# Sizing TensorE's fill-in work in an attention and MLP kernel: when ScalarE's bank comes free, what runs first as a round ends, and an early half of the last projection

## The chip, the cores and the metric

The kernel runs on one core of a Trainium2 chip. The metric is the device time of one execution in microseconds (us). Before the change the median of three runs was 858.73 us (858.62 to 859.59). The span that a profile shows is some 1.8 us shorter than the time of the same run. Ratios are taken only between kernels that ran on the same chip in the same rounds.

Engines are named as the profile has them: PE is TensorE, DVE is VectorE, ACT is ScalarE, POOL is GpSimd, SP is SyncE. PSUM is the memory that TensorE writes its sums to; a piece of it that holds one tile of sums is called a bank here.

## The reference

One gate per token mixes the result of an attention block with that of an MLP block. All inputs are bf16.

```python
# x: (1, 2048, 512); 32 heads of 16
q, k, v = split_heads(x @ wqkv)
scores  = einsum("bhqd,bhkd->bhqk", q, k) * 16 ** -0.5
a = merge_heads(softmax(scores) @ v) @ wo

h  = gelu(layernorm(x) @ w1)                    # 512 -> 512
hs = shift_rows(h, by=(1, -1, 2, -2)) @ w2      # each quarter of the columns by its own shift
x1 = x + hs
b  = x1 + gelu(layernorm(x1) @ w3) @ w4         # 512 -> 1792 -> 512

g = sigmoid((x * gate_w).sum(-1))
return g * a + (1 - g) * b
```

Attention dominates: 32 heads times 2048 x 2048 scores. Each score needs an exponential, and no single engine could do all of them in time: at the 0.955 us that ScalarE takes for two tiles, the 2048 tiles would be 978 us of ScalarE (an estimate).

## The kernel before

The Python code holds a model of the engines. At build time it plays the program through, picks for each engine what to do next, and so lays down a fixed order of instructions; nothing is decided on the chip. Attention runs in 32 rounds (4 chunks of queries, 4 groups of 8 heads, 2 halves of a group), each of 64 score tiles of 128 x 512. A round's value matmuls sum into one PSUM bank, `acc`, which is copied out when the round ends; only then may the next round's value matmuls start, and only some ten of its score tiles may be issued ahead.

A score tile goes one of two ways. ScalarE takes two at a time and does a true exp. VectorE takes one at a time with a bit trick, then makes shifted copies (the third by POOL), so that four value matmuls together average out the trick's error. All other TensorE work is *fill-in*: the projections of attention and MLP, and value matmuls. It is put between the score groups. This is the heart of it, where TensorE picks its next work:

```python
def pe_pick():
    t = sim.t
    ...   # 1. scores, if a PSUM bank of ScalarE's or VectorE's is free and tiles may be issued
    if ops:
        sim.pe_run(ops)
        return True
    ...
    # 2. fill-in: how many passes of 216 ns?
    tr = sim.t_free["ACT"]                     # when ScalarE ends the instruction that it is at work on
    budget = tr - t - 95.0 + (SL[turn[0]])     # SL = (350, 350)
    if tr <= t:
        budget = 500.0
    n = int(budget // 216.0)
    if n <= 0:
        return False
    n = min(n, MAXU)                           # MAXU = 9
    ops = []
    g = gen_ready()                            # a projection whose inputs are there
    cnt = pv_counts()                          # value matmuls that are ready
    flush = n_left(min(acc_round[0], NR - 1)) == 0   # the round has no scores left to issue
    press = sum(cnt) > PRESS or len(sim.free["PA"]) <= PA_LOW or len(sim.free["PD"]) <= PD_LOW
    ...
    if g is not None and g.due <= sim.tiles:   # a projection that is due goes first, always
        do_gen()
    if press:
        do_pv(0.01)                            # value matmuls before projections
        do_gen()
    else:
        do_gen()
        if (len(ops) + 3) // 4 < n:
            do_pv(PV_FULL)
    if not ops and any(cnt):
        do_pv(0.01 if flush else PV_IDLE)
```

Two other places matter. The gate's sixteen columns are stored so that every element is on its own:

```python
d1 = dma(2200.0, [a], lambda: nc.sync.dma_start(
    out=zE_dram[:].rearrange("(t p) -> p t", p=P), in_=zE[:]))
```

And at the end, between the copy of the last sums and the steps that normalise them, TensorE does projections of the last chunk, which wait for nothing that is new:

```python
nc.scalar.copy(out=ab[:, 256:512], in_=acc[:, 256:512])
nc.vector.tensor_copy(out=ab[:, 0:256], in_=acc[:, 0:256])
for b in range(4):
    nc.tensor.matmul(pd[:, 4*b:4*b+4], lhsT=ab[:, b*P:(b+1)*P], rhs=idf[:, 0:P:32], start=True, stop=True)
# before these, in TensorE's order: last_gen(0..2); after them last_mms(3):
# each one fp32 identity matmul (adds y) and four passes with wo, G = 0..3
```

The whole kernel before:

The softmax here doesn't subtract the row's maximum and nothing guards it: scores larger than these inputs give would overflow.

## Time and profile before

| | before |
|---|---|
| span of the profiled run | 858.7 us |
| mean granted clock of TensorE | 0.962 |
| busy: PE, DVE, ACT, POOL | 93%, 91%, 86%, 44% |
| exp pairs on ScalarE | 717 |
| bit-trick tiles on VectorE | 615 |
| ScalarE idle ahead of its exps | 100.5 us |
| last copy of sums to the end | 14.7 us |

The lines of the page that carry this are in the prediction. How they are read: a group's line has the busy time, the mean time of one in ns, and then the idle time of that engine just before these instructions with what ended most of it. The waits give, for one waiting line and one releaser, the total, the number of times and the longest. A timeline line has start, length, engine and line, what it does, how many in a row, and in brackets how long the engine had been idle and what released it.

One thing that the prediction tells only by numbers is better seen. This is the timeline of before at a place with projections:

```profile
684.10 2.12 PE L495 MATMUL ring<-w,hT 128*32 128x512 bf16 x36
686.16 0.39 PE L789 MATMUL psA<-q,kT 32*128 32x512 bf16 x2
686.65 1.94 ACT L866 ACTIVATE PA<-psA 128x1024 bf16<-128x1024 f32 x2 [0.71 <-PE ring L789]
```

Thirty-six matmuls, four side by side, are nine passes. They take 2.12 us. ScalarE has two banks, each good for one exp of about 0.95 us, so it runs dry in that time and stands for 0.71 us until scores come again. When that run of fill-in ends both banks are empty.

The old budget counts until the instruction that ScalarE is at work on ends, and adds a quarter of a microsecond. The plan, built again with its picks printed, shows how nine passes come of it: they are three picks in a row, of two, three and four passes. The first is made while the model has ScalarE idle, the second during the first exp. The third comes just after that exp has ended; in the model its bank is free only 160 ns later, so no score can be issued yet, and the budget now counts to the end of the second exp, which already runs. While a GELU runs, the budget is cut only by `MAXU`.

### The profile page before, as it was taken

To read this page: it belongs to the slowest core of one execution; us is meant where nothing else is said; L and a number is where in the kernel's file an instruction comes from. 1 tells how busy PE (TensorE), PEld (TensorE's weight loads), DVE (VectorE), ACT (ScalarE), POOL (GpSimd) and SP (SyncE) were. 2 spreads that over 40 slices of the span, in tenths; PEclk is the share of its full clock that TensorE was granted. 3 is DMA by queue.
4 is the path that set the end of the run, shared out by engine and by line. 5 is a ranking of instruction groups with operands and counts; after the bars stand their busy time and mean duration, and the time that the engine had idled before them with its cause. 6 is when DMAs were issued, how large, how long until landed. Compare 5 with 4: busy or idle time off the path is not lost.

```text
span 858.7 us, 24104 instructions
## 1 busy us (share of the span) xinstructions
PE 794.5 (93%) x9715; PEld 253.8 (30%) x9715; DVE 785.6 (91%) x1657; ACT 735.1 (86%) x743; POOL 379.6 (44%) x369
## 2 busy tenths in 40 slices
PE   8979999998999898979999998999989999979987
PEld 3423333222222222222232232332222332222323
DVE  6978999998999999997969998999999989989893
ACT  6867788989899897998958998789999779999883
POOL 3243444444444453443524544344555534445442
PEclk9988999997899999998999997999989999989999
DMA  9212222113002232011000002101100100000000
GB/s 223 77 34 56 61 55 47 38 40 103 6 18 66 65 102 64 9 39 39 15 28 26 19 18 43 34 12 27 34 18 18 31 24 13 16 17 19 15 18 29
DMA packets 67016, 34.62 MB, mean 40 GB/s; under 512 B 46684, under 2 KB 62300, under 8 KB 66904
## 3 DMA queue, kind: packets, MB, share of 16 engines
q1 hardware_dynamic: 65288, 32.29, 14.9%
q8 instruction: 76, 1.25, 0.6%
q10 hardware_dynamic: 1616, 0.79, 0.3%
q14 instruction: 36, 0.29, 0.1%
HBM read 17.39 MB, written 6.81 MB: 28 GB/s over the span
## 4 chain that ended last, share of the span: by engine, by line
PE 41%; DVE 36%; ACT 11%; issue 5%; DMA 5%; SPq 1%; ACTq 0%; POOL 0%; DVEq 0%; POOLq 0%
PE acc L954 15%; PE ring L495 14%; DVE PD L891 14%; DVE PD L920 11%; PE psA L789 11%; ACT PA L866 7%; ACT hT L707 2%; DMA pk<-den 2%; DVE st L616 2%; DMA zE_dram<-zE 1%; DVE accsb L970 1%; DVE hT L706 1%; DVE x_sb L685 1%; DVE V L579 1%; DVE xn L636 1%
## 5 line engine op out<-in xcount | busy, mean ns | idle before, releaser
L866 ACT ACTIVATE PA<-psA 128x1024 bf16<-128x1024 f32 x717 | 684.4, 1029 | 100.5 <-PE ring L789 51.6
L923 POOL TENSOR_SCALAR PD<-PD 128x1024 uint16<-128x1024 uint16 x308 | 326.1, 1060 | 446.4 <-DVE PD L920 298.1
L891 DVE TENSOR_SCALAR PD<-ring 128x512 uint16<-128x512 f32 x615 | 400.9, 679 | 26.9 <-PE ring L789 18.9
L954 PE MATMUL acc<-PD,V 128*17 128x512 bf16 x2460 | 339.5, 395 | 21.1 <-DVE PD L920 7.4
L789 PE MATMUL psA<-q,kT 32*128 32x512 bf16 x1433 | 270.7, 392 | 23.8 <-ACT PA L866 22.4
L954 PE MATMUL acc<-PA,V 128*17 128x512 bf16 x1433 | 283.4, 388 | 0.4 <-DVE accsb L970 0.4
L920 DVE TENSOR_SCALAR PD<-PD 128x1024 uint16<-128x1024 uint16 x616 | 260.5, 464 | 1.8
L789 PE MATMUL ring<-q,kT 32*128 32x512 bf16 x615 | 201.7, 398 | 5.9 <-DVE PD L891 5.5
L789 PEld LDWEIGHTS <-kT 32*128 32x128 bf16 x2048 | 72.6, 91 | 286.0 <-issue 284.0
L954 PEld LDWEIGHTS <-V 128*17 128x17 bf16 x3893 | 94.3, 89 | 199.9 <-issue 160.8
L495 PE MATMUL ring<-xnT,w 128*32 128x512 bf16 x1152 | 84.8, 382 | 1.6 <-DVE PD L891 1.3
L495 PE MATMUL ring<-w,hT 128*32 128x512 bf16 x1152 | 81.3, 388 | 1.1 <-DVE PD L891 0.9
L495 PEld LDWEIGHTS <-w 128*32 128x32 bf16 x1920 | 45.3, 96 | 49.6 <-issue 32.9
L987 POOL TENSOR_TENSOR oT<-accsb,bcs 128x512 bf16<-128x512 f32 x31 | 40.6, 1311 | 9.4 <-DMA bcs<-rr 9.4
L495 PEld LDWEIGHTS <-hT 128*32 128x32 bf16 x1152 | 28.3, 97 | 37.7 <-issue 19.2
L706 DVE CAST hT<-ring 128x512 bf16<-128x512 f32 x56 | 38.1, 681 | 1.3 <-PE ring L495 0.9
L495 PE MATMUL ring<-w,w 128*32 128x256 bf16 (+1 forms) x768 | 36.2, 316 | 0.7 <-DVE PD L891 0.4
L707 ACT ACTIVATE hT<-hT 128x7168 bf16<-128x7168 bf16 x4 | 24.7, 6177 | 0.0
L970 DVE COPY accsb<-acc 128x512 f32<-128x512 f32 x31 | 21.1, 679 | 2.7 <-PE acc L954 2.7
L616 DVE BATCH_NORM_STATS2 st<-x_sb 128x6 f32<-128x512 bf16 x32 | 21.8, 681 | 0.0
L495 PE MATMUL ring<-wo,oD 128*32 128x512 bf16 x240 | 20.9, 380 | 0.0
L495 PE MATMUL ring<-w,wq 128*32 128x512 bf16 x256 | 18.4, 382 | 2.3 <-DVE PD L891 1.4
(82 smaller groups left out, 203.5 us busy)
## 6 DMA issues: line engine op xcount, KB each, us to landing
bcs<-rr SPq DMA_DIRECT2D x124, 64.0 KB
xn_dram<-xn SPq DMA_DIRECT2D x32, 128.0 KB
w<-in_B_w_dram SPq DMA_DIRECT2D x5, 512.0 KB
oD<-oT SPq DMA_DIRECT2D x124, 16.0 KB
w<-in_B_w_dram SPq DMA_DIRECT2D x4, 448.0 KB
out_dram<-ot SPq DMA_DIRECT2D x13, 128.0 KB
x_sb<-in_A_x_dram SPq DMA_DIRECT2D x3, 512.0 KB
w<-in_A_wqkv_dram SPq DMA_DIRECT2D x2, 256.0 KB
```

Of the source, the lines that this page charges most:

```text
L495: units.append([Op("col", j, lambda j=j, lf=lf, rf=rf, n0=n0, n1=n1, st=st, sp=sp: nc.tensor.matmul(get()[32 * j:32 * j + 32, n0:n1], lhsT ...
L616: a = dve(600, deps, lambda: nc.vector.bn_stats(out=sb.slot[:], in_=x_sb[:, t, :]), prio=6, at=at, acq=[sb])
L706: pre.append(evac(g, PSUM_NS, lambda ps, m=m: nc.vector.tensor_copy(out=h2[:, m, :], in_=ps[:])))
L707: ge = act(93 + 427 * FT + 2600, pre, lambda: nc.scalar.activation(out=h2, in_=h2, func=ACT.Gelu_apprx_tanh), prio=0)
L789: o = Op("row", i, lambda: nc.tensor.matmul(dst(), lhsT=kT[G][32 * i:32 * i + 32, kt * P:(kt + 1) * P], rhs=qbuf[G, c].slot[32 * i:32 * i ...
L866: job = act(hold, ops, lambda: nc.scalar.activation(out=pb.slot[:, 0:n], in_=buf.slot[:, 0:n], func=ACT.Exp, scale=0.25), acq=[pb], frees= ...
L891: nc.vector.tensor_scalar(out=pr["buf"].slot[:, h * 512:(h + 1) * 512], in0=buf.slot[:], scalar1=BITS_MUL, scalar2=BITS_ADD, op0=ALU.mult, ...
L920: nc.vector.tensor_scalar(out=d[k][:, 0:w], in0=d[0][:, 0:w], scalar1=float(SHIFT * k), scalar2=None, op0=ALU.add)
L923: nc.gpsimd.tensor_scalar(out=d[k][:, 0:w], in0=d[0 if both else 2][:, 0:w], scalar1=1.0, scalar2=float(SHIFT * (k if both else 1)), op0=A ...
L954: o = Op("col", i, lambda: nc.tensor.matmul(acc[32 * i:32 * i + DH + 1, :], lhsT=lhs(), rhs=rhs(), start=st, stop=True, tile_position=(0, ...
L970: e = dve(PSUM_NS, round_ops[r], lambda: nc.vector.tensor_copy(out=ab.slot[:], in_=acc[:]), acq=[ab], prio=0)
L987: n = gp(1250, d3, lambda: nc.gpsimd.tensor_tensor(out=ob.slot[:], in0=ab.slot[:], in1=bb.slot[:], op=ALU.mult), acq=[ob], frees=[ab, bb], ...
```

## The change

It has four parts and a new set of constants (with them some of the model's prices for work of VectorE and for transfers):

1. The *size of fill-in*: counted until the earliest exp that has started gives its bank back (its end plus 160 ns), plus 60 ns; 508 ns, or two passes, while no exp is at work. It no longer reaches on into the next exp or through a GELU.
2. The *round-end rule*: once a round has no scores left to issue, ready value matmuls go before projections, even before due ones.
3. The *gate's store* is transposed on TensorE first, so that it leaves as 16 rows of 512 bytes.
4. The *end*: half of the last chunk's projection sums go into the earlier w4 groups, and what remains is spread around the small matmuls. VectorE makes the third copies itself as a round ends.

The core of the diff, with cuts marked:

```diff
-    SL = (350, 350)
+    SL = (60, 60)
+    IDLE_NS = 508
+    FLUSH = 1
 ... # some twenty constants retuned: priorities, due times, caps (P1_PRIO, PA_LOW, DVE_CAP, PRESS, MAXU, P_W2, ...)
@@ the gate
-        d1 = dma(2200.0, [a], lambda: nc.sync.dma_start(out=zE_dram[:].rearrange("(t p) -> p t", p=P), in_=zE[:]))
+        gt = gen("z", at, [a, j_idf], [])
+        gt.units = [[Op("full", None, lambda: nc.tensor.matmul(gt.buf.slot[0:NT, 0:P], lhsT=zE[:], rhs=idf[:], ...
+        ec = dve(200, gt.ops, lambda: nc.vector.tensor_copy(out=zT(), in_=gt.buf.slot[0:NT, 0:P]), ...
+        d1 = dma(2200.0, [ec], lambda: nc.sync.dma_start(out=zE_dram[:].rearrange("(t p) -> t p", p=P), in_=zT()), frees=[zb])
@@ issue_act
+        exps[:] = [j for j in exps if j.done is None]
 ...
+        exps.append(job)
@@ close_pair: VectorE makes all copies when few scores of the round are left
+        alone = n_left(rl) <= (URG_L if rl == NR - 1 else URG)
@@ pe_pick
-        tr = sim.t_free["ACT"]
-        budget = tr - t - 95.0 + (SL[turn[0]])
-        if tr <= t:
-            budget = 500.0
+        tr = min((j.start + j.hold + j.lat for j in exps if j.start is not None and j.done is None), default=None)
+        budget = tr - t + SL[turn[0]] if tr is not None else IDLE_NS
 ...
-        if g is not None and g.due <= sim.tiles:
+        if g is not None and g.due <= sim.tiles and not flush:
             do_gen()
-        if press:
+        if press or flush and FLUSH:
             do_pv(0.01)
             do_gen()
@@ the w4 groups of the last chunk, and the end
+            ng = 4 if c < NCH - 1 else LG          # LG = 2
 ...
+    known(0)
+    known(1)
     for b in range(4):
         nc.tensor.matmul(pd[:, 4 * b:4 * b + 4], ...
+    known(2)
+    known(3)
```

## The prediction

> **What bounds the kernel now.** I read busy time first, then the groups, the waits, and then the stretches in which one engine is full and another is not. Busy time by engine (us, share of the span, instructions):
>
> ```profile
> PE 794.5 (93%) x9715; PEld 253.8 (30%) x9715; DVE 785.6 (91%) x1657; ACT 735.1 (86%) x743; POOL 379.6 (44%) x369
> ```
>
> Three engines are nearly full; POOL is not and may be forgotten. The work is 2048 score tiles. ScalarE takes 1433 of them, two at a time (exp); VectorE takes 615, one at a time (bit trick), and then makes shifted copies of each pair. TensorE feeds both and multiplies by V: one value matmul for a ScalarE tile, four for a VectorE tile. The groups give the prices:
>
> ```profile
> L866 ACT ACTIVATE PA<-psA 128x1024 bf16<-128x1024 f32 x717 | 684.4, 1029 | 100.5 <-PE ring L789 51.6
> L891 DVE TENSOR_SCALAR PD<-ring 128x512 uint16<-128x512 f32 x615 | 400.9, 679 | 26.9 <-PE ring L789 18.9
> L954 PE MATMUL acc<-PD,V 128*17 128x512 bf16 x2460 | 339.5, 395 | 21.1 <-DVE PD L920 7.4
> L920 DVE TENSOR_SCALAR PD<-PD 128x1024 uint16<-128x1024 uint16 x616 | 260.5, 464 | 1.8
> ```
>
> Busy time over count is the price in a full pipeline: 684.4/717 = 0.955 us for an exp pair, 400.9/615 = 0.652 for a VectorE tile, 260.5/616 = 0.423 for a copy. The reader should see that ScalarE, the engine with room, is idle 100.5 us ahead of its exps, and that the releaser is a score matmul. The waits say so again (total, times, longest):
>
> ```profile
> ACT PA L866 <- PE ring L789: 51.6, 85, 3.1
> ACT PA L866 <- PE psA L789: 38.7, 34, 8.7
> ```
>
> Thus 90 us of ScalarE's idle time are TensorE coming late while it does fill-in (projections and value matmuls). For TensorE, busy is not occupancy, so I made a ledger from a timeline:
>
> ```profile
> 421.86 0.39 PE L789 MATMUL psA<-q,kT 32*128 32x512 bf16 x2
> 422.18 0.83 PE L495 MATMUL ring<-w,hT 128*32 128x512 bf16 x12
> 422.94 0.39 PE L789 MATMUL psA<-q,kT 32*128 32x512 bf16 x2
> ```
>
> Up to four matmuls run side by side in one pass. Nine passes elsewhere span 2.06 us with the last end included, (2.06-0.38)/8 = 0.21, so I use 0.216. One score pass takes 0.32 to the next start, three fill passes 0.76: each change between score and fill mode costs 0.10 to 0.11, I use 0.105. The built program has 2752 passes and 1293 changes: 594.4 + 135.8 = 730.2 us. The granted clock is 0.962 on the mean, 0.038 x 858.7 = 32.6 us lost. TensorE is thus truly idle for about 96 us, and is the second engine, not the first. VectorE, idle 73 us, is first. Where it is not full, the stretches tell (us, then busy of PE, PEld, DVE, ACT, POOL, granted clock, DMA share, GB/s):
>
> ```profile
> 52.00:78.00 26.00, 20.08 (x229) 6.38 (x226) 17.11 (x40) 16.53 (x17) 9.51 (x10) 0.79 0.22 39
> 104.00:130.00 26.00, 23.77 (x313) 7.81 (x309) 26.00 (x55) 21.00 (x23) 10.72 (x11) 1.00 0.21 55
> 364.00:390.00 26.00, 19.58 (x213) 5.38 (x205) 22.36 (x45) 24.98 (x20) 11.69 (x11) 0.88 0.14 32
> 416.00:442.00 26.00, 25.64 (x360) 8.88 (x352) 18.35 (x40) 17.08 (x19) 9.94 (x10) 1.00 0.08 23
> ```
>
> The second row is the usual one: VectorE full, ScalarE 81%. The third holds a GELU, the fourth long projections. The first has a stall of its own (timeline):
>
> ```profile
> 52.13 0.39 SPq L606 DMA_DIRECT2D zE_dram<-zE  x1
> ...
> 63.59 0.69 DVE L891 TENSOR_SCALAR PD<-ring 128x512 uint16<-128x512 f32 x1 [5.55 <-remote]
> 63.62 4.97 ACT L866 ACTIVATE PA<-psA 128x1024 bf16<-128x1024 f32 x5 [5.59 <-remote]
> ...
> 64.69 0.61 PE L789 MATMUL psA<-q,kT 32*128 32x512 bf16 x2 [4.79 <-ACT PA L866]
> ```
>
> The gate's 8 KB go out from 52.13, and the chain of waits has them under way for 11.54 us. VectorE and ScalarE stop together and start again as they land; then matmuls last 0.60 instead of 0.39 until about 72.6.
>
> **What the Trainium skill says.** "TensorE: Matmul & The Clock Gate", Part 1, What's actually happening: after an idle window of about 3.4 us TensorE drops to half clock, and about as long a busy stretch restores it. The trace agrees: 0.39 becomes 0.60 after 4.79 us of idling here and after the first GELU (208 to 234 us has clock 0.77). "DMA: Bandwidth & Descriptors", Rules for kernel authors: a non-contiguous last dimension becomes one descriptor per element. The zE store is of that shape, and 11.54 us for 8 KB agrees. "TensorEngine Tiling (Array Packing)", PSUM Bottleneck: tiling speeds up TensorE, not the emptying of PSUM. Agreed: 0.652 us to empty a tile against a shared 0.216 us pass.
>
> **The change part by part.** Counts are from the instruction order of the two built programs.
>
> (1) *Tiles move.* Exp pairs go from 717 (716 whole) to 733, VectorE tiles from 615 to 582, copies from 616 to 586. VectorE: 33 x 0.652 = 21.5, 28 x 0.423 plus two half ones = 12.4, against about 0.9 for two more gate products and one small copy: net -33.0, so 752.6. ScalarE: 17 x 0.955 less the half exp = +15.6, so 750.7. POOL falls by about 22 and stays far off.
>
> (2) *Fill-in.* Its runs between two score groups were 115 of one pass, 216 of two, 173 of three and 139 of four or more, the last holding 947 passes; they become 19, 448, 197 and 64, these holding 433. A score pass, two fill passes and two changes take 0.216 + 0.432 + 0.21 = 0.86 us, under the exp's 0.955; three take 1.07; nine take 2.37 and starve both readers of PSUM. That is how ScalarE gets its 16 pairs. The price: 1461 mode changes, +168 x 0.105 = +17.6 us; passes fall to 2694 (99 fewer value matmuls, fuller passes), 58 x 0.216 = -12.5. Ledger 735.3, so +5 for TensorE.
>
> (3) *The gate's store* is transposed on TensorE first, 16 rows of 512 B. It removes the 5.6 us stall and most of what follows it at low clock (ScalarE waits 3.1 us once there): -8.6.
>
> (4) *The end.* From 844.04, where the last sums are copied, to 849.07, where the next step's matmul starts, TensorE does last projections. Half of them now sit in the w4 groups, and two of four identity matmuls went. What stays ahead is four passes and one fp32 identity: 4 x 0.216 + 0.86 = 1.7 us instead of 5.0: -3.3.
>
> (5) *GELUs.* Between the score pairs that bracket the five GELUs TensorE had 160 value or fill matmuls, now 254, 23 passes more in time when it idled. The clock should fall less: of 32.6 us lost, 5.5 are the gate's stall (0.21 x 26), and of the other 27 I take a third away. On the path perhaps -6.
>
> (6) *Value matmuls first at a round's end* and VectorE making all copies there shorten waits of 7.0 us (acc for its copy) and some of VectorE's: at most 3, counted in the range only.
>
> **The sum, in two ways.** By VectorE: 752.6 + idle 73.1 less 8.6, 3.3 and about 3 = 810.8. By TensorE: 735.3 + clock loss 18 + idle 96 less 4.8, 3.3 and 5 = 836. The middle is 823. The three engines come out equal (752.6, 750.7, 753), and equal engines wait more for one another, so I add 4: 827 us, 3.7% under 858.7.
>
> **Rivals.** (A) *TensorE takes over*: the 168 changes land just where VectorE was the bound, its relief is not used, and the time is 836 to 848. For it: the ledger rises, and the fourth stretch above is TensorE's alone. Against: 96 us idle, of which the change uses some. (B) *Only the stall and the tail count*: the tiles moved merely shift idle time, 858.7 - 11.9 = 847. For it: VectorE's low stretches are at GELUs and projections, which stay. Against: in the usual stretch VectorE is busy 26.00 of 26. (C) *VectorE's relief is paid in full*: 810 to 815. (D) *The plan slips*: order is fixed when built, so if real waits come in other places the short runs make TensorE stand before full banks, 855 to 870. For it: new constants shift everything; against: the plan's new hold times are nearer the profile's.
>
> **Range and chances.** C sets the low end, 812; A with part of B the high end, 845. Faster by over 2% means below 841.6: C, the middle and half of A, 0.79. Within 2%: the rest of A, B, part of D: 0.18. Slower: 0.03.
>
> **What would show it.** Right: VectorE busy near 753 and ScalarE near 751, each 90 to 92%; exp's idle time under 75 us; no stall near 50 to 65 us; under 2.5 us from the last copy to the next matmul; mean clock above 0.97. Wrong: TensorE's waits vanish while the chain shows over half PE (A); exp's idle stays near 100 (B, D); the clock falls although fill-in was spread.

## The result

The changed kernel takes 806.82 us in the median of four runs (804.37 to 807.62), against 858.67 (855.41 to 859.59) for the kernel before. The ratio is 0.9398, with a 95% interval of 0.9366 to 0.9430: 6.0% faster. A ratio here is always the mean time of one kernel's fast runs over that of the other's of the same rounds, so it is not quite the ratio of the medians quoted. "Worth x us" means a difference of two such ratios times 858.7. The span of the profiled runs fell from 858.7 to 805.4 us.

The prediction was 827 us, with a range of 812 to 845. The direction was right. The range was missed on the fast side by 5 us.

Busy time of the changed kernel by engine, and its groups that answer to those shown of before:

```profile
PE 776.0 (96%) x9602; PEld 226.6 (28%) x9602; DVE 751.4 (93%) x1597; ACT 738.2 (92%) x759; POOL 355.4 (44%) x348
```

```profile
L884 ACT ACTIVATE PA<-psA 128x1024 bf16<-128x1024 f32 x733 | 687.4, 1039 | 48.1 <-PE psA L804 27.5
...
L910 DVE TENSOR_SCALAR PD<-ring 128x512 uint16<-128x512 f32 x582 | 383.1, 681 | 23.9 <-PE ring L804 20.5
L980 PE MATMUL acc<-PD,V 128*17 128x512 bf16 x2328 | 316.0, 386 | 14.8 <-DVE PD L946 6.2
...
L946 DVE TENSOR_SCALAR PD<-PD 128x1024 uint16<-128x1024 uint16 x586 | 242.1, 452 | 2.1
```

VectorE does 34.2 us less (785.6 to 751.4), ScalarE 3.1 us more, and ScalarE's idle time ahead of its exps halves, from 100.5 to 48.1 us. The waits say which half went:

```profile
ACT PA L884 <- PE psA L804: 27.5, 25, 4.6
ACT PA L884 <- PE ring L804: 10.8, 21, 0.9
```

The two lines must be read apart, and the rest of this document turns on it. "Ring" waits are the many short ones, in which a score group came late after a run of fill-in: 85 of them, 51.6 us, are now 21 with 10.8 us. "psA" waits are fewer, and the longest are among them: 34 with 38.7 us, the longest 8.7, are now 25 with 27.5 us, the longest 4.6. The name only tells which matmul of the score group came last, so the place of a wait must be looked at too. The three longest "psA" waits of before (8.7, 4.1 and 3.5 us) stand at ends of rounds; at GELUs there is hardly any (0.7 us). Counted in the traces by place, waits for scores with the copy of a round's sums beside them (from 1.5 us before the wait to 2.0 us after it) took 29.1 us before and take 18.8 now; all others took 61.5 us and take 19.5. The 4.6 us of the changed kernel lie in the first round; none at a round's end is over 1.9 us.

The gate's store. First the stretch in which it stalled before (columns as in the prediction), then the timeline of the changed kernel:

```profile
52.00:78.00 26.00, 25.33 (x343) 7.97 (x340) 24.67 (x58) 25.88 (x30) 11.82 (x12) 1.00 0.24 51
```

```profile
52.28 20.38 ACT L884 ACTIVATE PA<-psA 128x1024 bf16<-128x1024 f32 x22
57.72 0.32 SPq L621 DMA_DIRECT2D zE_dram<-ot  x1
```

ScalarE runs 22 exps in a row straight through the store. VectorE is busy 24.67 us of the 26 instead of 17.11, and the clock is 1.00 instead of 0.79. The packets under 512 B fell from 46684 to 44636, by 2048: one for each of the 16 x 128 values.

The end, on the timeline of before and then of the changed kernel:

```profile
844.04 0.37 ACT L1200 COPY accsb<-acc 128x256 f32<-128x256 f32 x1 [1.68 <-PE acc L954]
849.07 1.05 PE L1203 MATMUL psA<-idf,accsb 128*128 128x4 f32 x8
```

```profile
793.69 0.37 ACT L1230 COPY accsb<-acc 128x256 f32<-128x256 f32 x1 [0.52 <-PE acc L980]
795.40 1.05 PE L1235 MATMUL psA<-idf,accsb 128*128 128x4 f32 x8
```

From copy to matmul 5.03 us have become 1.71. From the copy to the end of the span it is 14.66 before (858.7 less 844.04) and 11.71 after: 2.95 us.

Last, the chain that ended last, by engine, before and then after:

```profile
PE 41%; DVE 36%; ACT 11%; issue 5%; DMA 5%; SPq 1%; ACTq 0%; POOL 0%; DVEq 0%; POOLq 0%
```

```profile
PE 63%; DVE 28%; DMA 3%; issue 3%; ACT 1%; POOL 1%; SPq 0%; ACTq 0%; DVEq 0%; POOLq 0%
```

ScalarE leaves the chain (11% to 1%), and TensorE's share rises to well over half. It is tempting to read from this that TensorE is the bound now. (In `after_replanned`, with the same rules in another order, the share is 53%.) The experiments test that.

Where the 53.3 us of profiled span (858.7 to 805.4) went, by the times at which each round's sums are copied out:

| stretch | before, us | after, us | gained |
|---|---|---|---|
| rounds 0 to 2 (start, gate's store) | 105.6 | 93.5 | 12.1 |
| the five rounds that hold GELUs | 154.8 | 150.7 | 4.1 |
| the 24 other rounds | 584.0 | 549.9 | 34.1 |
| after the last round's copy | 14.3 | 11.3 | 3.0 |

Most of it comes from the ordinary rounds: 24.3 us each on the mean before, 22.9 after, though single ones spread widely (21.0 to 32.3 us before, 18.3 to 29.6 after). The GELUs do not fall into the same five rounds in the two kernels.

### The profile page after: what moved, and what is told of

It reads as the page before. It is cut to its first block, busy times and chain, and to the rows that moved or that the text cites. A ratio compares the mean times of both kernels' runs of the same rounds, so it can differ in the third digit from the quotient of the medians.

```text
span 805.4 us, 23809 instructions
## 1 busy us (share of the span) xinstructions
PE 776.0 (96%) x9602; PEld 226.6 (28%) x9602; DVE 751.4 (93%) x1597; ACT 738.2 (92%) x759; POOL 355.4 (44%) x348
## 2 busy tenths in 40 slices
DMA packets 64982, 34.60 MB, mean 43 GB/s; under 512 B 44636, under 2 KB 60268, under 8 KB 64872
## 4 chain that ended last, share of the span: by engine, by line
PE 63%; DVE 28%; DMA 3%; issue 3%; ACT 1%; POOL 1%; SPq 0%; ACTq 0%; DVEq 0%; POOLq 0%
PE acc L980 22%; PE ring L502 20%; PE psA L804 19%; DVE PD L910 11%; DVE PD L946 10%; DMA pk<-den 2%; PE ring L804 1%; DVE st L631 1%; DVE x_sb L700 1%; DMA den<-accsb 1%; ACT hT L722 1%; DVE accsb L996 1%; DVE V L586 1%; DMA x_sb<-in_A_x_dram 1%; DVE kT L546 1%
## 5 line engine op out<-in xcount | busy, mean ns | idle before, releaser
L884 ACT ACTIVATE PA<-psA 128x1024 bf16<-128x1024 f32 x733 | 687.4, 1039 | 48.1 <-PE psA L804 27.5
L949 POOL TENSOR_SCALAR PD<-PD 128x1024 uint16<-128x1024 uint16 x287 | 301.5, 1051 | 416.8 <-DVE PD L946 294.4
L910 DVE TENSOR_SCALAR PD<-ring 128x512 uint16<-128x512 f32 x582 | 383.1, 681 | 23.9 <-PE ring L804 20.5
L980 PE MATMUL acc<-PD,V 128*17 128x512 bf16 x2328 | 316.0, 386 | 14.8 <-DVE PD L946 6.2
L804 PE MATMUL psA<-q,kT 32*128 32x512 bf16 x1466 | 281.0, 388 | 2.3 <-ACT PA L884 2.1
L980 PE MATMUL acc<-PA,V 128*17 128x512 bf16 x1466 | 274.4, 383 | 0.5 <-DVE accsb L996 0.5
L946 DVE TENSOR_SCALAR PD<-PD 128x1024 uint16<-128x1024 uint16 x586 | 242.1, 452 | 2.1
L980 PEld LDWEIGHTS <-V 128*17 128x17 bf16 x3794 | 78.5, 88 | 158.4 <-issue 134.0
L502 PE MATMUL ring<-xnT,w 128*32 128x512 bf16 x1152 | 95.5, 386 | 0.6 <-DVE PD L910 0.6
L502 PE MATMUL ring<-w,hT 128*32 128x512 bf16 x1152 | 93.8, 387 | 0.6 <-DVE PD L910 0.5
L502 PE MATMUL ring<-w,w 128*32 128x256 bf16 (+1 forms) x768 | 42.8, 315 | 0.3 <-DVE kT L546 0.3
L502 PEld LDWEIGHTS <-hT 128*32 128x32 bf16 x1152 | 24.9, 95 | 36.4 <-issue 28.6
L502 PE MATMUL ring<-wo,oD 128*32 128x512 bf16 x224 | 20.4, 383 | 0.0
L502 PE MATMUL ring<-w,wq 128*32 128x512 bf16 x256 | 20.4, 399 | 0.0
```

What stands on the lines that cost most here:

```text
L502: units.append([Op("col", j, lambda j=j, lf=lf, rf=rf, n0=n0, n1=n1, st=st, sp=sp: nc.tensor.matmul(get()[32 * j:32 * j + 32, n0:n1], lhsT ...
L804: o = Op("row", i, lambda: nc.tensor.matmul(dst(), lhsT=kT[G][32 * i:32 * i + 32, kt * P:(kt + 1) * P], rhs=qbuf[G, c].slot[32 * i:32 * i ...
L884: job = act(hold, ops, lambda: nc.scalar.activation(out=pb.slot[:, 0:n], in_=buf.slot[:, 0:n], func=ACT.Exp, scale=0.25), acq=[pb], frees= ...
L910: nc.vector.tensor_scalar(out=pr["buf"].slot[:, h * 512:(h + 1) * 512], in0=buf.slot[:], scalar1=BITS_MUL, scalar2=BITS_ADD, op0=ALU.mult, ...
L946: nc.vector.tensor_scalar(out=d[k][:, 0:w], in0=d[0][:, 0:w], scalar1=float(SHIFT * k), scalar2=None, op0=ALU.add)
L949: nc.gpsimd.tensor_scalar(out=d[k][:, 0:w], in0=d[0 if both else 2][:, 0:w], scalar1=1.0, scalar2=float(SHIFT * (k if both else 1)), op0=A ...
```

## The experiments

Eighteen kernels ran, all accepted in the comparison with the reference. An experiment that starts from the changed kernel is named `after_...` and has something undone; one that starts from before is named `before_...` and has something of the change added. The medians of before in the five sets were 859.4 to 862.43 us. The changed kernel was not run again in them: a difference from it compares two ratios taken on different chips, each to before on its own chip.

Where an edit alters how the order is laid down, the whole order moves, since it is planned anew. How much a new order by itself can move the time was measured too (`after_replanned`, below: 6.5 us, one sample), and differences of that size are not explained here.

### First set: which part carries it

The theory was that of the prediction: the size of fill-in carries most, the store and the end what the trace before showed of them, and the round-end rule little. The rival was that the round-end rule counts for much more than its 3 us.

**after_old_store.** The changed kernel with the old store; the order of the instructions is unchanged.

```diff
-  out=zE_dram[:].rearrange("(t p) -> t p", p=P), in_=zT()
+  out=zE_dram[:].rearrange("(t p) -> p t", p=P), in_=zE[:]
```

> The changed kernel with the gate's values stored element by element again (everything else, and the order on every engine, as it is; the transposition is still done, only not stored). Theory 1 (the element-wise store stops VectorE and ScalarE for some 5 us and lowers TensorE's clock after it): 8 to 12 us slower than the changed kernel, so 815 to 819 us, with a stall of about 5 us ended by a remote releaser in the trace after the store is issued. Rival (the store was hidden, the early gain comes from the other order): within 2 us of 806.8.

Measured: 819.14 us against 862.43, ratio 0.9494 (0.9462 to 0.9526), 8.2 us slower than the changed kernel. The size is right. The form of the stall is not quite that of before, in this timeline:

```profile
64.01 1.29 DVE L910 TENSOR_SCALAR PD<-ring 128x512 uint16<-128x512 f32 x2 [1.53 <-remote]
...
71.05 0.18 DVE L1004 TENSOR_TENSOR pk<-pk,gpk 128x16 f32<-128x16 f32 x1 [5.08 <-DMA gpk<-zE_dram]
```

VectorE stands 1.53 us with the same releaser, "remote", that ended the 5.55 us in before, but then 5.08 us for the gate's values to come back (2.85 us in before). The fixed order had put a small product that needs them at this place. A late transfer costs through whatever comes next in the order, not only where it runs.

"Remote" means that the program found no instruction for the release. The semaphores in the trace of before tell more: VectorE and ScalarE waited for TensorE's own. Five of its updates, by matmuls recorded as ended from 58.22 to 59.46, came only from 63.53 to 63.71, as the store landed (its last updates at 63.66 and 63.67). So TensorE's signal was late, or its matmuls ended later than recorded. What held it is not shown; that the store's shape brings it about, the next run shows.

**before_row_store.** The kernel before with a store whose rows are contiguous, and the values in the wrong places on purpose (the result still passed the comparison within its tolerance, so the comparison can't be used to tell that they are wrong).

```diff
-  out=zE_dram[:].rearrange("(t p) -> p t", p=P), in_=zE[:]
+  out=zE_dram[:].rearrange("(p t) -> p t", p=P), in_=zE[:]
```

> The kernel before, order unchanged, with the same 8 KB stored as 128 runs of 64 B instead of element by element. The result is wrong on purpose (the gate's values land in another order). Theory 1: 8 to 12 us faster than before, 847 to 851 us, no stall between 58 and 64 us and no clock of 0.79 in that stretch. Rival (the wait would be there anyway, for the next transfer): within 3 us of 858.7.

Measured: 852.27 us, ratio 0.9871 (0.9853 to 0.9890): 11.1 us faster with nothing but the store's shape changed. In the stretch from 52 to 78 us the clock is 0.96, VectorE is busy 25.48 us and ScalarE 22.82. So this part is worth 8 to 11 us, on both sides. Here 1920 fewer packets under 512 B go out, as 128 runs instead of 2048 values should give.

**after_late_projection.** The changed kernel with no early sums of the last projection.

```diff
-    LG = 2
+    LG = 0
```

> The changed kernel with no early part of the last projection: all four pieces of each of the last four tiles after the last value matmul, instead of two. The built order is otherwise nearly the same (2697 passes instead of 2694 in all). Theory 1 (the end is a chain, each pass ahead of the small transposing matmuls is paid): four passes of 0.216 more ahead of them, and four more after, of which two or so are covered: 0.9 to 1.7 us slower, about 808. Rival (the copies of the last sums take as long anyway): within 0.5 us.

Measured: 813.51 us, ratio 0.9422 (0.9385 to 0.9459). That is 2.1 us slower than the changed kernel, but the intervals overlap, so the time alone settles nothing. The trace does show the place: from the copy of the last sums to the next matmul it is 2.9 us instead of 1.7, and to the end 13.7 instead of 11.7.

**after_no_flush.** The changed kernel with the old order at a round's end.

```diff
-    FLUSH = 1
+    FLUSH = 0
-        if g is not None and g.due <= sim.tiles and not flush:
+        if g is not None and g.due <= sim.tiles:
```

> The changed kernel without the rule that value matmuls go first once a round's scores are all issued. Theory 1 (round ends were worth little: 12 waits of 7.0 us in all for the accumulator's copy): 2 to 6 us slower, 809 to 813. Rival 1 (round ends are a main part of the gain, since the value matmuls of the next round and the buffers behind them wait for the accumulator): over 12 us slower, above 819, with more idle time of TensorE ahead of value matmuls. Rival 2 (nothing): within 2 us.

Measured: 838.05 us, ratio 0.9727 (0.9693 to 0.9761). Two lines of ordering cost 28.3 us. My theory fell here, and the rival held. The waits of this kernel:

```profile
ACT PA L884 <- PE psA L804: 67.5, 34, 10.4
ACT PA L884 <- PE ring L804: 12.3, 22, 3.3
```

The short waits are as rare as in the changed kernel (12.3 us against 10.8). The long ones are back and worse than before the change: 67.5 us against 27.5. The timeline shows one of them, the longest:

```profile
668.79 0.39 PE L804 MATMUL psA<-q,kT 32*128 32x512 bf16 x2
...
671.50 3.19 PE L502 MATMUL ring<-w,hT 128*32 128x512 bf16 x56
674.52 1.03 PE L502 MATMUL ring<-wo,oD 128*32 128x512 bf16 x16
675.38 3.19 PE L502 MATMUL ring<-w,hT 128*32 128x512 bf16 x56
...
680.72 1.94 ACT L884 ACTIVATE PA<-psA 128x1024 bf16<-128x1024 f32 x2 [10.42 <-PE psA L804]
```

From 669 to 679 us TensorE does nothing but projections (w4 and wo), one after the other, while ScalarE waits 10.42 us. Here is the stretch as busy times:

```profile
672.00:681.00 9.00, 8.84 (x159) 4.03 (x152) 2.63 (x5) 0.28 (x1) 0.00 (x0) 1.00 0.09 31
```

TensorE is busy 8.84 of 9 us, and both its customers stand: VectorE 2.63, ScalarE 0.28. The share of busy time calls this TensorE at its best. Of the waits for scores of this kernel 59.4 us stand at ends of rounds, against 18.8 in the changed kernel; elsewhere it is 20.4 against 19.5. The expected sign of the rival, more idle time of TensorE ahead of value matmuls, hardly came (18.6 us against 15.3): TensorE was not idle but busy with other work. All these projections fell due at a round's end, when no score could be issued until the round's value matmuls were done; and due projections went before value matmuls. The changed kernel with its rule, at the end of one of its rounds, with projections at hand:

```profile
599.69 0.60 PE L502 MATMUL ring<-xnT,w 128*32 128x512 bf16 x3
600.03 0.69 DVE L996 COPY accsb<-acc 128x512 f32<-128x512 f32 x1
600.65 3.77 ACT L884 ACTIVATE PA<-psA 128x1024 bf16<-128x1024 f32 x4 [0.53 <-PE ring L804]
```

The round closes (the copy at 600.03) with three projection matmuls beside it, and ScalarE has waited 0.53 us. At the end of the very round of the 10.42 us (number 25, counted from 0) it waits 1.07 us.

### Second set: the size of fill-in and the constants, on both sides

**after_old_budget.** The changed kernel with the old way of counting.

```diff
-    SL = (60, 60)
+    SL = (350, 350)
-        tr = min((j.start + j.hold + j.lat for j in exps if ...), default=None)
-        budget = tr - t + SL[turn[0]] if tr is not None else IDLE_NS
+        tr = sim.t_free["ACT"]
+        budget = tr - t - 95.0 + (SL[turn[0]])
+        if tr <= t:
+            budget = 500.0
```

> The changed kernel with only the old size of the fill-in (until ScalarE's present instruction ends, plus 255 ns, and everything that fits while a GELU runs). In the built order the runs of four passes or more hold 1076 passes instead of 433, the mode changes fall from 1461 to 1292, and passes rise from 2694 to 2874, since value passes go less full. Theory 1 (the size of the fill-in is the main part of the gain): 25 to 45 us slower, 832 to 852, ScalarE idle ahead of its exps 90 us or more instead of 48. Rival (the spread of the projections over the rounds, by the constants, is the main part): less than 12 us slower, under 819.

Measured: 848.59 us against 861.33, ratio 0.9854 (0.9839 to 0.9869), 39.2 us slower. The waits:

```profile
ACT PA L884 <- PE ring L804: 55.6, 99, 4.8
ACT PA L884 <- PE psA L804: 27.3, 45, 1.7
```

This is the mirror image of the last run. The long waits stay cured (no "psA" wait over 1.7 us), and the short ones are all back: 99 of them, 55.6 us.

**before_new_budget.** The kernel before with the new way of counting only.

```diff
-    SL = (350, 350)
+    SL = (60, 60)
+    IDLE_NS = 508
 ... # and the new tr and budget, as in the change
```

> The kernel before with only the new size of the fill-in (until the next bank of ScalarE comes free, plus 60 ns; 508 ns while none is due). Order: 1427 changes instead of 1293, 2702 passes instead of 2752, 504 passes in runs of four or more instead of 947. Theory 1: 20 to 35 us faster than before, 824 to 839, ScalarE's idle time ahead of its exps under 65 us. Rival (constants): less than 10 us faster, above 849. Rival of the prediction (mode changes make TensorE the bound and eat it): no faster at all.

Measured: 847.12 us, ratio 0.9835 (0.9820 to 0.9850): 14.2 us faster, where taking the same thing out of the changed kernel cost 39.2. It fell short of what I had expected, and the waits say why:

```profile
ACT PA L870 <- PE psA L790: 55.6, 28, 12.7
ACT PA L870 <- PE ring L790: 18.8, 34, 4.3
```

Short waits fell from 51.6 to 18.8 us, as they should. Long waits grew from 38.7 to 55.6 us, and the longest from 8.7 to 12.7. Counted by place, waits elsewhere fell from 61.5 to 22.9 us and those at the ends of rounds rose from 29.1 to 51.6. More than half of what was gained was handed back there.

**after_old_constants** has the changed kernel's rules with the constants of before; **before_new_constants** is the opposite. The edit is the block of constants alone.

```diff
-    P1_PRIO = 0.414
+    P1_PRIO = 0.475
 ... # QAT, QDUE, PA_LOW, DVE_CAP, AHEAD, PV_IDLE, PRESS, MAXU, DUES, P_W1 to P_W4, P_V, P_V2, P_G, P_LD
```

> The changed kernel (new fill-in size, round ends, store, end) with the old planning constants: when each projection may start, priorities, how far a round may run ahead, pressure limits. Order: 1467 changes, 2672 passes. Theory 1 (constants are a small part): 3 to 12 us slower, 810 to 819. Rival (constants are the main part): over 20 us slower.

> The kernel before with only the new planning constants. Order: 1288 changes, 2877 passes. Theory 1 (constants were tuned for the new fill-in and do nothing or harm without it): between 5 us faster and 15 us slower than before, 854 to 874. Rival (constants are the main part): over 15 us faster, under 844.

Measured: 818.20 us, ratio 0.9510 (0.9488 to 0.9532), 9.6 us slower than the changed kernel; and 867.43 us, ratio 1.0074 (1.0057 to 1.0091), 6.4 us slower than before. The constants by themselves bring nothing; they fit one set of rules. In the first of the two kernels one hole stands out on the timeline:

```profile
446.40 1.94 ACT L884 ACTIVATE PA<-psA 128x1024 bf16<-128x1024 f32 x2 [14.94 <-PE acc L980]
```

One wait of 14.94 us, where w3 and w4 work meets the end of round 16. The changed kernel has no wait for `acc` of ScalarE's over 3.0 us, and that one is at the same round's end. The hole comes with both rules and the old constants: `before_budget_flush` (fourth set) has it too, with 12.25 us, while the three later variants with the new constants have 3.1 to 5.3 us there. It alone is as large as the 9.6 us. So the new constants may be worth just this hole; no run takes out the due times alone, and the cause of the hole is not shown.

### Third set: is there one engine that bounds?

If one engine were the bound, work added to it would be paid in full, and work added to another engine not at all. In two kernels each, every twelfth bit-trick instruction was done twice (VectorE), or every fifth pair of scores (TensorE). The order of all else was left alone.

```diff
+            dn[0] += 1
+            for _ in range(2 if dn[0] % 12 == 0 else 1):     # ..._more_vector
                 nc.vector.tensor_scalar(out=pr["buf"].slot[:, h * 512:(h + 1) * 512], in0=buf.slot[:], ...
+        dn[0] += 1
+        if dn[0] % 5 == 0:                                   # ..._more_tensor
+            ops[-1].fn = lambda fs=[o.fn for o in ops]: (fs[-1](), [f() for f in fs])
```

> The kernel before, order unchanged, with every 12th of VectorE's emptyings of a score tile done twice: 51 x 0.652 = 33 us more for VectorE, same result. Theory 1 (in the kernel before VectorE set the pace and TensorE's 96 us of idle time were mostly spent waiting on it, so VectorE's time is paid nearly in full): 22 to 33 us slower. Rival (the prediction's second sum: TensorE's time and its idle time stand by themselves): under 12 us slower.

> The kernel before, order unchanged, with every 5th pair of score matmuls for ScalarE done twice into the same banks: 140 more passes of 0.216 us = 30 us more for TensorE, same result. Theory 1 (TensorE has slack that belongs to VectorE): 6 to 15 us slower. Rival (TensorE is the bound as much as VectorE): over 20 us slower.

> The changed kernel, order unchanged, with every 12th emptying done twice: 48 x 0.652 = 31 us more for VectorE. Theory 1 (after the change the bound has moved towards TensorE, whose share of the chain rose from 41 to 63%): 12 to 22 us slower, less than the same did to the kernel before. Rival (VectorE still sets the pace): 25 us or more.

> The changed kernel, order unchanged, with every 5th pair of score matmuls done twice: 144 more passes of 0.216 us = 31 us more for TensorE. Theory 1 (TensorE is now the bound, 55 us of idle time left): 18 to 28 us slower, clearly more than the same did to the kernel before. Rival: under 12 us, as before.

| kernel | added work (an estimate) | ratio (95%) | slower by | paid |
|---|---|---|---|---|
| before_more_vector | 51 x 0.652 = 33 us | 1.0263 (1.0238 to 1.0288) | 22.6 us | 68% |
| before_more_tensor | 140 passes x 0.216 = 30 us | 1.0211 (1.0193 to 1.0229) | 18.1 us | 60% |
| after_more_vector | 48 x 0.652 = 31 us | 0.9688 (0.9652 to 0.9724) | 24.9 us | 80% |
| after_more_tensor | 144 passes x 0.216 = 31 us | 0.9656 (0.9639 to 0.9673) | 22.2 us | 71% |

Two of the four miss the numbers expected (TensorE in before and VectorE in the changed kernel both cost more), and a third, TensorE in the changed kernel, lies within its numbers, but at 22.2 us is not clearly above the 18.1 us that the same cost in before, as it should have been. Instead the two cost much the same in both, and in each kernel the two shares add up to more than 100%. Of these two engines neither is *the* bound, and the 63% that TensorE has in the chain after the change does not make it one. An engine's idle time here reads best as time in a chain that passes through all three engines, not slack that belongs to one. Two limits: ScalarE got no added work, and TensorE's stood right ahead of exps, so its share holds for that place. Why the shares are 60 to 80%, rather than other values, stays open.

### Fourth set: do the two rules need each other?

The theory by now ("theory 2") was that ScalarE's waiting has two causes, that each rule cures one, and that short runs alone make the second worse, because projections put off pile up until a round's end. The rival was that each rule has a worth of its own, and the sums just happen to differ. The two-by-two on both sides tells them apart.

**before_flush_only** has the round-end rule alone, **before_budget_flush** both rules and nothing else of the change, **after_neither** everything but these two.

```diff
-        if g is not None and g.due <= sim.tiles:
+        if g is not None and g.due <= sim.tiles and not flush:
             do_gen()
-        if press:
+        if press or flush:
```

> The kernel before with only the round-end rule (value matmuls first once a round's scores are all issued). Order: 1255 changes, 2764 passes, still 615 VectorE tiles; the longest stretches without an exp pair fall from 43, 22 and 19 passes to 14, 12 and 12, but 84 stretches of six passes or more remain (64 before). Theory 2 (round ends become costly only with short fill-in runs, since the old runs work off most projections before the round's end; the two parts need each other): between 3 us slower and 8 us faster than before, so about 853 to 864. Rival (the round-end rule is worth its 28 us by itself): 20 us or more faster, under 841.

> The kernel before with the new size of the fill-in and the round-end rule, and nothing else of the change. Order: 732 exp pairs and 584 VectorE tiles (the changed kernel has 733 and 582), 1457 changes, 2682 passes. Theory 2: more than the sum of the two alone (14.2 us for the size, about 0 to 8 for the rule), 30 to 42 us faster than before, 819 to 831; the rest of the change then is the gate's store (8 to 11), the end (2 to 3) and the constants. Rival (parts add up): 14 to 22 us faster, 839 to 847.

> The changed kernel with the old size of the fill-in and without the round-end rule; the store, the end and the constants stay. Order: 1308 changes, 2854 passes, 613 VectorE tiles. Theory 2 (without the short runs the rule is worth little): within 8 us of the kernel with the old size alone, so 842 to 857 (ratio 0.976 to 0.995). Rival (the rule is worth 28 us by itself): 870 or more.

Measured: 855.12, 825.61 and 847.60 us, against 859.40. Ratios: 0.9957 (0.9931 to 0.9983), 0.9597 (0.9577 to 0.9617), 0.9860 (0.9833 to 0.9887). With the runs above, in us against the corner kernel of each side:

| | starting from before | starting from the changed kernel |
|---|---|---|
| neither rule | 0 | +39.7 |
| round-end rule only | -3.7 | +39.2 |
| new fill-in size only | -14.2 | +28.3 |
| both | -34.6 | 0 |
| both, if each had only its own worth | -17.9 | -11.9 from "neither" |
| what they bring only together | 16.7 | 27.8 |

The single entries are good to 1 to 3 us, so the last row is far outside the scatter of the timing, and on both sides outside the 6.5 us by which a new order alone moved the time. That is one sample, though, and each entry is a new order, so the size of the last row is rough. What settles the cause is where ScalarE waits for scores, counted by place as above (us):

| | before: at round ends | before: elsewhere | changed: at round ends | changed: elsewhere |
|---|---|---|---|---|
| neither rule | 29.1 | 61.5 | 25.1 | 59.6 |
| round-end rule only | 13.9 | 73.7 | 15.9 | 67.0 |
| new fill-in size only | 51.6 | 22.9 | 59.4 | 20.4 |
| both | 12.4 | 18.8 | 18.8 | 19.5 |

On both sides the new size cures most of the waits elsewhere and about doubles those at round ends, and the rule cures these. (`before_budget_flush` waits another 26.4 us for `acc`, 12.25 of them in the hole told of above.)

The round-end rule alone is worth next to nothing (3.7 and 0.5 us), and on top of the new fill-in size 20.4 and 28.3 us. Its waits, when alone in before, are these:

```profile
ACT PA L866 <- PE ring L789: 66.7, 107, 5.3
ACT PA L866 <- PE psA L789: 20.9, 37, 1.9
```

The long waits are cured (the longest is 1.9 us instead of 8.7), but the short ones grow from 51.6 to 66.7 us: the projections that may not run at a round's end now run in full nine-pass stretches in the middle. Counting the passes that TensorE runs without a score pair for ScalarE in between shows it too (start and GELUs left out): the three longest such stretches are 43, 22 and 19 passes in before, 63, 47 and 32 in before_new_budget, 14, 12 and 12 in before_flush_only, and 24, 15 and 12 in the changed kernel. But before_flush_only has 84 stretches of six passes or more, and the changed kernel 21. Each rule on its own pushes the projections to the other place.

**after_replanned.** The same rules with a slightly different allowance, to see what a new order alone does.

```diff
-    SL = (60, 60)
+    SL = (50, 50)
```

> The changed kernel with the slack of the fill-in set to 50 instead of 60 ns: a change too small to matter for itself, after which the planner lays the whole order anew (736 exp pairs, 576 VectorE tiles, 1469 changes, 2680 passes). It shows how far a new order alone moves the time, against which 10 us for the old constants are to be judged. If re-planning is harmless: within 5 us of the changed kernel (ratio 0.934 to 0.946). If orders scatter: 8 us or more away.

Measured: 814.42 us, ratio 0.9474 (0.9459 to 0.9488): 6.5 us slower than the changed kernel. The constants' 9.6 us are hardly more than this, so how much of that is their merit and how much is luck of order can't be told.

### Fifth set: is there a better version?

**after_long_idle_run** lets TensorE do more fill-in when ScalarE is not at work at all; **after_vector_third_copy** has VectorE make some more third copies.

```diff
-    IDLE_NS = 508
+    IDLE_NS = 720      # after_long_idle_run
-    GP3 = 1.0
+    GP3 = 0.85         # after_vector_third_copy
```

> A try for a better version: the changed kernel with three passes instead of two per fill-in run while no exp is due (720 ns for 508), which matters only in GELUs. Order: 736 exp pairs, 576 VectorE tiles, 1465 changes, 2690 passes; stretches of six passes or more without an exp pair hold 146 passes instead of 186. If fewer long stretches are worth their passes: 3 to 6 us faster than the changed kernel, ratio 0.933 to 0.937. If it is only another order, as the replanned one was: 0.938 to 0.950.

> Another try: the changed kernel with VectorE making the third shifted copy too for 15 pairs in 100 (POOL makes it otherwise, 1.05 us a copy and later). Order: 740 exp pairs, 567 VectorE tiles, 1473 changes, 2688 passes. VectorE: 15 fewer tiles x 0.652 = 9.8 less, about 7 fewer pairs x 2 x 0.42 = 6 less, some 42 third copies x 0.42 = 18 more: about equal. If the late third copy holds up rounds: faster, ratio under 0.936. If not: 0.938 to 0.950 as any new order.

Measured: 808.69 us, ratio 0.9381 (0.9339 to 0.9424), and 811.94 us, ratio 0.9413 (0.9362 to 0.9464), both against 860.15. These are 1.5 us faster and 1.3 us slower than the changed kernel, with overlapping intervals. No version better than the changed kernel is shown.

## Why the prediction was right or wrong

**(1) Tiles move: right for VectorE, too high for ScalarE.** VectorE's busy time is 751.4 us for 752.6 predicted. ScalarE's is 738.2 for 750.7, because the price of an exp pair is not fixed. In the timelines shown, two in a row take 1.94 us, four 3.77 and 22 take 20.38, while one by itself takes about 1.02 in the traces. Each exp that follows another directly thus adds about 0.92. With fewer waits more of them do, and the mean price fell from 0.955 to 0.938 us.

**(2) The size of fill-in: right in kind.** ScalarE's idle time ahead of its exps is 48.1 us, under the 75 given as the sign, and the short waits fell as described. The 168 extra mode changes did not bring rival A: its sign (PE over half of the chain) came, its time (836 to 848 us) did not. So that sign was a bad one: work added to TensorE was paid at 71%, to VectorE at 80%.

**(3) The store: right.** 8.6 predicted; 8.2 and 11.1 measured from the two sides.

**(4) The end: right by the traces.** 3.3 predicted; 2.95 in the traces. The 1.7 us from copy to matmul came to 1.71. The time of `after_late_projection` does not show this part by itself.

**(5) GELUs: agrees, not isolated.** The clock's loss is 0.019 x 805.4 = 15.3 us, where 18 was predicted, and the five rounds with GELUs gained 4.1 us, where 6 was. No run took this part out by itself. One reading in the prediction was wrong: it takes the half clock after the first GELU for the effect of an idle window. In the trace of before the clock fell at 206.06 us, and in the 3.41 us before that TensorE was busy for 1.90 us, with no pause over 0.83 us; at the four other GELUs no pause was over 1.37 us. The case that agrees is the pause of 4.79 us at the store.

**(6) Value matmuls first at a round's end: this step failed.** The prediction said "at most 3, counted in the range only". It measured 28.3 us when taken out of the changed kernel, and 20.4 when put on top of the new fill-in size in before (0.9835 less 0.9597). I had priced the rule by TensorE's twelve waits of 7.0 us in all for the copy of `acc`, in the trace of before. ScalarE's waits for scores at round ends, 29.1 us in the same trace, I had not counted: the 8.7 us that the prediction shows as the longest "psA" wait is one of them, and I read past it. And the rule's main work is to stop a harm that the other part does: with short runs, projections pile up until a round ends, and those waits grow to 51.6 us. That growth is not in the trace of before; it comes with the change.

**The sum: the ledger's idle term failed too.** Counted by TensorE the sum was 836, with idle time of 96 us falling to 83. It fell to 805.4 - 735.3 - 15.3 = 54.8. The 4 us added "because equal engines wait more for one another" went the wrong way. The sum by VectorE, 810.8, came nearest, with idle time of 54.0 us (805.4 less 751.4) where about 58 was assumed. I took the middle of two sums that both treated idle time as belonging to an engine, to be carried over less a few named pieces. The third set speaks against that. Of the 21.6 us between 827 and the span of 805.4, 12.6 come from taking the middle, 4 from the added term, and 5 were left in the sum by VectorE. That this sum came near is partly luck: it carried VectorE's idle time over without asking what keeps it down. Without the round-end rule, and with VectorE busy for much the same time, that idle time is 70.9 us (`after_no_flush`, 836.8 less 765.9).

**What adds up and what doesn't.** Both rules 34.6, store 8.2 to 11.1, end about 3: 46 to 49 us of the 51.7 (0.0602 x 858.7). The rest, 3 to 6 us, lies with the constants and prices of the model, the copies at round ends and the luck of the order, and is not resolved.

## What to carry to other kernels

When filler work is made smaller in one place, ask where it will collect, and what has priority there; two rules that bring 14 and 4 us alone may bring 35 together, and a trace of the kernel before shows only the harm already there. Split a total wait by length and by place before pricing a change; here the short ones in the middle and the long ones at round ends had different causes. When three engines are over 85% busy, neither the fullest one nor the one with the largest share in the chain need be the bound: add a known amount of work to each and see what is paid.

## What the Trainium skill lacked or had wrong

- "Perfetto Trace Analysis", Identifying the Most-Contended Engine, says to optimize the engine with the highest occupancy first (TensorE apart, which it does not judge by busy time). That is VectorE here, with 91%. It was not enough: added work was paid in part on VectorE (22.6 of 33 and 24.9 of 31 us) and on TensorE (18.1 of 30 and 22.2 of 31 us) alike, and the largest gain, 34.6 us, came from two rules on what TensorE does next. The page's next section asks for the gaps on the engine being optimized and what ended them; here those of ScalarE told, the least busy of the three (86%). The page has no advice to add work as a test.
- "TensorEngine Tiling (Array Packing)", Key Properties, says that a change of tiling mode drains TensorE, without a figure. In this kernel a change between score passes and fill-in passes costs 0.10 to 0.11 us, by the starts in the prediction's timeline and its 0.216 us a pass.
- "DMA: Bandwidth & Descriptors", Rules for kernel authors, is right on the element-wise store (2048 fewer packets without it), but nothing in these rules says that engines with no part in the transfer may stand. Here VectorE and ScalarE stopped for 5.6 us, waiting for TensorE's signals, which came as the store landed, and an 8 KB store cost the kernel 8.2 to 11.1 us by its shape alone.
- No page says how little work is enough to halve TensorE's clock. At the five GELUs of before it fell with no pause of TensorE over 1.37 us, after 3.41 us with 1.1 to 2.3 us of work.
